# Two tiny weight reads ahead of ScalarE's table load, and the last two x tiles sent by ScalarE behind it

## The chip, the core and the metric

The kernel runs on one core of a Trainium2 chip. The metric is the device time of one execution in microseconds (us); lower is better. The engines are named as the profile names them: PE (TensorE, matrix products; PEld its weight loads), DVE (VectorE), ACT (ScalarE), POOL (GpSimd) and SP (SyncE, which here only issues transfers). ACT can issue transfers too, from a queue of its own (ACTq in the profile; SP's is SPq).

## The reference

One input x of 2048 tokens by 512 features goes through two branches, and a gate per token mixes them. Everything is bf16.

```python
x = A_x
g = sigmoid((x * gate_w).sum(-1, keepdims=True))
a = A_ref(x, wq, wk, wv, wo, beta)   # 32 heads of 16, 4 segments of 512 tokens:
                                     # softmax attention inside the segment, plus
                                     # a linear memory carried over the segments
b = B_ref(x, W_gate, W_up, W_down)   # relu(x @ W_gate) * (x @ W_up) @ W_down, F = 1792
return g * a + (1 - g) * b
```

What matters here is the very first step: q = x @ wq for the first 512 tokens, which needs x transposed (features on the partitions) and wq, both read from HBM.

## The kernel before

The program is recorded as a list of operations, each with the tiles it reads and writes. A scheduler class (`Sched`) places them one by one: the string `ORDER` holds one letter per operation, and each letter names a queue whose next operation is placed. From the tiles that an operation reads and writes, `add` derives what it must wait for, and `_waits` writes these waits into the engine's program, ahead of the instruction. Every engine runs its own program strictly in order, so an instruction that waits holds up all that stands behind it on that engine, transfers that it issues included. A transfer that writes a tile also waits for an earlier transfer into a tile of the same name (`need(t, False)` for each `t` in `r.dmaw`). Each transfer takes one of 16 semaphores (`s_dma0` to `s_dma15`), and the 17th use of one waits for the landing of the first.

The start of the program goes like this. The first 512 tokens of x are read as four tiles of 128 tokens (`load_x0(0)` to `load_x0(3)`, 128 KB each, into slots of the tile `hT`). PE turns each tile over in four 128x128 products with an identity (L449), and DVE and ACT copy the result from PSUM to `xT` (L454 and L456). Then PE computes q for the first segment in 32 matmuls of 256 columns (L552; the order of their pieces is set in `proj`): for each of the four 128-row pieces kt of wq, one matmul for each of four head groups. The 256 columns are either tokens 0 to 255 (x tiles 0 and 1) or 256 to 511 (x tiles 2 and 3). PE's order is: tiles 0 and 1 turned over; first token half with kt 0, then kt 1; tile 2 turned over; first half with kt 2; tile 3 turned over; first half with kt 3; then 16 matmuls for the second half. After that come k (L561), v (L559), the attention, and the feed-forward branch (L754).

SP reads x tiles 0 and 1, three pieces of wq, x tile 3, the fourth piece of wq, then wk, wv and the rest. ACT first loads its function table (a dummy `exp`, called "tab", which writes `rden` and so makes the table load happen early), and behind that it issues x tile 2: `load_x0(..., "act")` reads `rden`, so the transfer waits for "tab". Later ACT issues three tiny reads of 16 rows by 32 columns from the feed-forward weights into the tile `adT`, which is not used yet at that time; they are called `touch`. A queue of PE matmuls on constants (L441, L473) runs while the first tiles are on the way.

Of the kernel before, what the change touches and what calls it, by code (L numbers as in the profile page):

```python
# [21 lines left out]

LETTERS = "abcdefghijklmnopqrstuvwxyzABCDEFGHIJKLMNOPQRSTUVWXYZ0123456789"
ORDER = (
    "hafgbgbgfgbgfgbgfagbgfbhhhhgbhhhhijijhbttttbttttbhhhhijttttbhhhhijttttbttttcbtttbtDCttbttDbttbttbbtCbtbtFtbctIbItFbtbFJqbJtzJJtbEtxbtStGbvtGbzTvJtbMTq"
    "HtbJxvSbvSvbMvvcToqkvbLvoxtMTvbTvGTvlLvboqvoxvVMTvTvMTvTnlqVnvLoTvlxTMtWTtMmtTWtCTpqFvlSxtJtVJvTCvTtMyTVtTRqFvRtxvMTvJvpMvKTtSqzCvTTvMxTteMtrSeFTqATvx"
    "TvJetATttMeDTqJvxATtRvETvTvMyTqrAMTvxVQvAtrMUVUzATqUtAxTtpATtUtGTtHATqGvTxTvAtRtAvdHqMTtxTvATtTJttCTLqTvEKTtToxvdtvMTptCvTtSLqTErxSvAVtAtzTtTCvVTqATvM"
    "xtAdtRvEtLotdqAvpxCTtvTETvvTMKvTJqLvATxTvMvTdtMrzoqTpAvTxWvAvWMvtALTtAtHAqHvTAxTvosuPTMunTuPnpPqTuTxoXuTusuPuPTqPTOuTpJxuJTuuuXTquTxTsYuTPtPtPuTHXqTNu"
    "xYusvPuyPTuPTupTyRqXuuxSuTSvrNLTRqYuATxTJvATvvJvATvRLqvAxSuovMTvpTuMLvTqTArxuVQTvAUrUMTVBquATxuToutATpvTqSvxuATVtMTvUGvTOqVAvMTxvUAvYvJvMTKqTvoxvvMTpv"
    "TeMvTvTALvTeMqTvxTMvevBvMroeMTnqnvTxpATvvTAvovMTvATqLMvTxTvAvpMsvPtALtPTqADvTTxvPTtBtMrFTqTKJWvAxtWvAvtMvTDAtMTqTtAxtRtETvCtTtAvFtATLqTtBxtCTXttEtTsHu"  # L30
    "TPPTuPTqvXxJuJupvuMTquTxTsuTPuPtPtOTXqTGsxvPuPYPvuXyTMvTqTyRuuovxuTMpurRRqTAuxTtATuTJvtNKTuTGYTuATvouLqAprAxrQAUuUAUuBqtATxvUAtTouvHApqTAuxuuATTNuTvTB"
    "YvvMTLqTovxuMTvvuMnTqnpuToxJsuJPTuPvTPuTqTOvTvxYTMvpvMvvMTqvTxvMvsMvvTPqPTLvPTxvTvMvrMTqTAvTxvTAvMvvALTqAvxAvvMTTvMvTqTArTxMvBWAvWvTLAqTvxTAvAMTvvAvLq"
    "TAvTxMvTvTBvvMXTqvMTxTvXMTuuTquTxTuTuusvTPuPTMquxPuNXuuTqYrTxTTvAuAuTvTAuTLAqvAxuTAuuNTqYvTxTvMTvuMuTuTqrxvAuAvTuTAvTAvAqLuTxvuvNuYTuTvTMqTvMxvMvuuMTs"
    "qTPuPxTvPTuvXvMTvTvMTvTvLuqvxvMvvBvMTqvTAxuMvvNvLTvBYqrMTxTTvAvAvLTvTMvTvATLvAqAvxMvvAwMvTvBvMTwLTvTvvMvwLwrvAwAwwAwAvAwMwwAwwBwwwOwYOwwYwwwwwwOwwwYww"
    "wwwwwOwwwwwYNY"
)
BANKS = (
    "012312301230123023012302130231201320132013201301230210321032102310231023023020302013120312131213212301230213021301303120312031201201212012302301231231"
# [260 lines left out]
def build_kernel(nc, A_x, A_wq, A_wk, A_wv, A_wo, A_beta, W_g, W_u, W_d, gate_w, out):  # L299
    _, S, D = A_x.shape  # L300
    F = W_g.shape[1]
    assert D == 512 and S % 512 == 0 and F % 128 == 0
    NSEG, KT, NF, NT = S // 512, D // 128, F // 128, S // 128
    EPS, SCALE = 1e-6, 16 ** -0.5
    sc = Sched()
    T = {}
    with contextlib.ExitStack() as stack:
        for name, shape, dt in plan(S, D, F):
            T[name] = stack.enter_context(nc.sbuf_tensor(name, shape, dt))
        PL = stack.enter_context(nc.psum_tensor("psL", [128, 4, 512], F32))  # L310
        PA = stack.enter_context(nc.psum_tensor("psA", [128, 4, 512], F32))
        for st in sc.streams:
            sc.sem[st] = stack.enter_context(nc.semaphore(f"s_{st}"))
        program(sc, nc, T, PL, PA, A_x, A_wq, A_wk, A_wv, A_wo, A_beta, W_g, W_u, W_d, gate_w, out, NSEG, KT, NF, NT, EPS, SCALE)
        with nc.Block() as block:
            sc.emit(block)
    return sc


def program(sc, nc, T, PL, PA, A_x, A_wq, A_wk, A_wv, A_wo, A_beta, W_g, W_u, W_d, gate_w, out, NSEG, KT, NF, NT, EPS, SCALE):  # L320
    V = type("V", (), T)
# [16 lines left out]
    def act(fn, occ, **k):  # L338
        return op("act", fn, occ, **k)
# [15 lines left out]
    def load(eng, names, dst, src, nbytes, occ=460.0, reads=()):  # L355
        (lact if eng == "act" else lsp).append(dma(eng, lambda e, dst=dst, src=src: e.dma_start(dst, src), nbytes, occ=occ, reads=reads, writes=names, name="ld" + names[0]))  # L356
    x0 = A_x[0, 0:512, :].rearrange("(i p) d -> p i d", p=128)
    def touch(n, src):
        load("act", ["adT"], V.adT[0:16, 32 * n:32 * n + 32], src, 1024)
    def load_x0(i, eng="sp"):  # L360
        load(eng, [f"hT{i}"], V.hT[:, i, :], x0[:, i, :], 140000, reads=["rden"] if eng == "act" else [])

    def load_w(nm, w, src, kts):
        for kt in kts:
            load("sp", [f"{nm}{kt}"], w[:, kt, :], src[kt * 128:(kt + 1) * 128, :], 360000 if (nm, kt) == ("wk", 0) else 140000)
    load_x0(0)
    load_x0(1)
    load_w("wq", V.wq, A_wq, range(3))
    load_x0(3)
    load_w("wq", V.wq, A_wq, range(3, KT))  # L370
    lact.append(act(lambda e: e.activation(V.rden[:, 0:1], nc.const_aps.tensor(1.0, [128, 1], F32), ACT.Exp), 1500, writes=["rden"], name="tab"))
    load_x0(2, "act")
    sc.queue(0, lact)
    load_w("wk", V.wk, A_wk, range(KT))
    load_w("wv", V.wv, A_wv, range(KT))
# [529 lines left out]
```

## Time and profile before

| | |
|---|---|
| median of 3 runs | 264.53 us (264.4 to 264.64) |
| the profiled execution | 264.83 us |
| its span, from the first to the last instruction | 262.9 us |
| PE busy | 259.4 us, 99% of the span |
| DVE, ACT, POOL busy | 72%, 71%, 47% |
| HBM read and written | 9.87 MB and 2.11 MB |

All times inside the program count from the start of the span. A row of the timeline gives the start, the duration, the engine, the line of the kernel, the operation, its output and input tiles, and how many instructions were merged into the row; a bracket gives idle time ahead of it and what ended it. A row for a transfer's issue gives the time that the issuing queue was busy with it; when the data is there is told by the "us to landing" of the list of transfers, counted from the start of the issue.

### The profile page before, as it was taken

What the parts mean: (1) busy time and instruction counts of PE and PEld (TensorE: products, weight loads), DVE (VectorE), ACT (ScalarE), POOL (GpSimd) and SP (SyncE); (2) the same over time, 40 slices, a digit from 0 to 9 for tenths busy, and PEclk for the clock granted to TensorE, in tenths of its full rate; (3) what the DMA queues carried; (4) which work ended last, traced back from release to release, by engine and by line L of the source; (5) the groups of instructions that cost most, each with busy time, mean ns of one, the idle gap of its engine ahead of it and who ended that gap; (6) DMA issues with size and microseconds to landing.
All of it is one profiled execution on the core that took longest, in us unless ns stands there. A gap on an engine that the chain in (4) does not pass through costs nothing.

```text
span 262.9 us, 6637 instructions
## 1 busy us (share of the span) xinstructions
PE 259.4 (99%) x2761; PEld 115.5 (44%) x2761; DVE 189.3 (72%) x365; ACT 186.2 (71%) x163; POOL 122.7 (47%) x283
## 2 busy tenths in 40 slices
PE   8999999999999999999999999999999999999996
PEld 5543444434444444434444444444434444444444
DVE  4589878888894597888885898758973665577600
ACT  3598889888886877887876957777886755674021
POOL 3017645863655547845444456535654543343000
DMA  6979621533632311533212211010230000000011
GB/s 177 294 288 243 145 46 42 143 99 50 213 107 43 82 42 42 101 79 25 53 34 62 61 42 39 24 24 4 42 85 20 28 17 20 20 22 0 2 40 42
DMA packets 34685, 19.36 MB, mean 74 GB/s; under 512 B 24032, under 2 KB 34144, under 8 KB 34656
## 3 DMA queue, kind: packets, MB, share of 16 engines
q1 hardware_dynamic: 34416, 18.80, 28.6%
q8 instruction: 22, 0.36, 0.6%
q10 hardware_dynamic: 240, 0.13, 0.2%
q14 instruction: 7, 0.06, 0.1%
HBM read 9.87 MB, written 2.11 MB: 46 GB/s over the span
## 4 chain that ended last, share of the span: by engine, by line
PE 96%; DMA 1%; SPq 1%; issue 0%; DVE 0%
PE psA L754 39%; PE psA L793 19%; PE psA L561 9%; PE psL L662 9%; PE psA L694 7%; PE psA L786 5%; PE psA L559 5%; DMA wq<-in_A_wq_dram 1%; PE psA L624 1%; SPq L356 1%; PE psA L552 1%; PE psA L604 1%; DVE osb L802 0%
## 5 line engine op out<-in xcount | busy, mean ns | idle before, releaser
L671 POOL TENSOR_SCALAR_AFFINE_SELECT E<-E 64x256 bf16<-64x256 bf16 (+1 forms) x256 | 115.0, 459 | 115.4 <-ACT E L666 106.9
L666 ACT ACTIVATE E<-psL 128x2048 bf16<-128x2048 f32 x72 | 135.1, 1876 | 33.6 <-PE psL L662 33.2
L754 PE MATMUL psA<-xT,wu 128*128 128x512 bf16 x224 | 61.5, 380 | 0.0
L754 PE MATMUL psA<-xT,wg 128*128 128x512 bf16 x224 | 61.5, 380 | 0.0
L793 PE MATMUL psA<-wd,hT 128*128 128x512 bf16 (+2 forms) x238 | 58.8, 367 | 0.0
L765 DVE TENSOR_TENSOR hT<-psA,rl 128x512 bf16<-128x512 f32 x56 | 38.0, 682 | 15.1 <-PE psA L754 11.2
L793 PEld LDWEIGHTS psA<-wd,hT 128*128 128x128 bf16 x238 | 21.4, 98 | 24.3 <-issue 2.8
L754 PEld LDWEIGHTS psA<-xT,wu 128*128 128x128 bf16 x224 | 19.8, 98 | 25.2 <-issue 4.1
L754 PEld LDWEIGHTS psA<-xT,wg 128*128 128x128 bf16 x224 | 20.1, 98 | 24.4 <-issue 2.6
L704 DVE STREAM_TRANSPOSE Tn<-psA 128x512 f32<-128x512 f32 x32 | 21.4, 699 | 10.9 <-PE psA L694 10.6
L662 PE MATMUL psL<-qT,kp 32*128 32x192 bf16 (+7 forms) x512 | 28.7, 287 | 0.2 <-issue 0.2
L762 ACT ACTIVATE rl<-psA 128x512 bf16<-128x512 f32 x29 | 17.3, 596 | 15.0 <-PE psA L754 14.8
L763 DVE TENSOR_SCALAR rl<-psA 128x512 bf16<-128x512 f32 x27 | 18.5, 686 | 5.8 <-PE psA L754 5.6
L662 PEld LDWEIGHTS psL<-qT,kp 32*128 32x128 bf16 x512 | 8.3, 92 | 27.3 <-issue 9.7
L694 PE MATMUL psA<-E,vaug 64*17 64x128 bf16 (+7 forms) x512 | 18.7, 283 | 0.0
L694 PE MATMUL psA<-E,vsh 64*17 64x128 bf16 (+7 forms) x512 | 18.3, 283 | 0.0
L559 PE MATMUL psA<-wv,xT 128*128 128x512 bf16 x64 | 16.9, 379 | 0.0
L561 PE MATMUL psA<-xT,wk 128*128 128x512 bf16 x64 | 16.9, 379 | 0.0
L786 PE MATMUL psA<-wo,oT 128*128 128x512 bf16 (+2 forms) x68 | 16.5, 367 | 0.0
L803 ACT ACTIVATE osb<-psA,omg 128x512 bf16<-128x512 f32 (+1 forms) x8 | 5.4, 673 | 14.4 <-PE psA L786 13.1
L802 DVE TENSOR_SCALAR osb<-psA,omg 128x512 bf16<-128x512 f32 (+1 forms) x9 | 6.3, 702 | 12.5 <-PE psA L786 10.4
L694 PEld LDWEIGHTS psA<-E,vaug 64*17 64x17 bf16 x512 | 11.6, 86 | 7.6 <-issue 2.3
(73 smaller groups left out, 235.0 us busy)
## 6 DMA issues: line engine op xcount, KB each, us to landing
vsh<-vaug SPq DMA_DIRECT2D x8, 272.0 KB, 3.6
out_dram<-osb SPq DMA_DIRECT2D x15, 128.0 KB, 1.7
wg<-in_B_W_gate_dram SPq DMA_DIRECT2D x8, 224.0 KB, 5.4
wu<-in_B_W_up_dram SPq DMA_DIRECT2D x8, 224.0 KB, 5.9
osb<-in_A_x_dram SPq DMA_DIRECT2D x12, 128.0 KB, 2.2
wd<-in_B_W_down_dram SPq DMA_DIRECT2D x3, 512.0 KB, 4.5
wq<-in_A_wq_dram SPq DMA_DIRECT2D x4, 128.0 KB, 2.7
wk<-in_A_wk_dram SPq DMA_DIRECT2D x4, 128.0 KB, 3.5
```

Of the source, the lines that this page charges most:

```text
L559: ins = e.matmul(A(ep)[:, :], lhsT=V.xT[:, kt, tok + col * 128:tok + (col + 1) * 128], rhs=w[:, kt, :], start=(kt == 0), stop=(kt == KT - 1))
L561: ins = e.matmul(A(ep)[:, :], lhsT=w[:, kt, col * 128:(col + 1) * 128], rhs=V.xT[:, kt, tok:tok + 512], start=(kt == 0), stop=(kt == KT - 1))
L662: ins = q.matmul(PL[:, jj, o:o + 512 - 64 * c], lhsT=V.kp[r, kslot(s, G), c, :], rhs=V.qT[r, qslot(s, G), 64 * c:512], start=True, stop=Tr ...
L666: acts.append(act(lambda a: a.activation(V.E[:, e, :, :], PL[:, :, :], ACT.Exp, scale=SCALE), t_act(2048), reads=[f"bankL{b}" for b in ran ...
L671: pools.append(pool(lambda g, ap=ap, base=base: g.affine_select(out=ap, in_=ap, compare_op=ALU.is_ge, fill=0.0, base=base, pattern=[[0, 4] ...
L694: ins = q.matmul(A(eps[p])[32 * jj:32 * jj + 17, 64 * c:512], lhsT=v[:, 8 * G + 2 * jj + p, :], rhs=V.E[r, e, jj, o:o + 512 - 64 * c], sta ...
L704: ds.append(dve(lambda e, p=p, ep=eps[p]: e.transpose(V.Tn[:, p, :], A(ep)[:, :]), 706, writes=[f"Tn{p}"], name=f"tr{s}_{G}_{p}", ep=eps[p ...
L754: ins = e.matmul(A(ep)[:, :], lhsT=w[:, kt, f * 128:(f + 1) * 128], rhs=V.xT[:, kt, c * 512:(c + 1) * 512], start=(kt == 0), stop=(kt == K ...
L763: ("dve", lambda e, ep=eg, r=r: e.tensor_scalar(V.rl[:, r, :], A(ep)[:, :], 0.0, None, ALU.max), t_dve(512))],
L765: evs.append(dve(lambda e, ep=eu, r=r, hs=hs: e.tensor_tensor(V.hT[:, hs, :], A(ep)[:, :], V.rl[:, r, :], ALU.mult), t_dve(512), reads=[f" ...
L786: ins = e.matmul(A(ep)[:, 0:c1 - c0], lhsT=V.oT[:, o0 + G, i * 128:(i + 1) * 128], rhs=V.wo[:, G, c0:c1], start=st_ and G == 0, stop=sp_ a ...
L793: ins = e.matmul(A(ep)[:, 0:c1 - c0], lhsT=V.hT[:, slots[f], i * 128:(i + 1) * 128], rhs=V.wd[:, f, c0:c1], start=st_ and f == f0, stop=sp ...
```

## The change

The change writes the start of the loads in another order. ACT's queue gets two tiny reads, of 16 rows by 32 columns of wq and of wk, ahead of the table load. x tile 3 moves from SP to ACT, behind x tile 2. SP, without x tile 3, sends the four pieces of wq in a row. The table `ORDER` gets letters for the two added operations and the moved one.

```diff
-    "hafgbgbgfgbgfgbgfagbgfbhhhhgbhhhhijijhbttttbttttbhhhhijttttbhhhhijttttbttttcbtttbtDCttbttDbttbttbbtCbtbtFtbctIbItFbtbFJqbJtzJJtbEtxbtStGbvtGbzTvJtbMTq"
+    "haaafgbgbgfgbgfgbgfagbgfahhhhgbhhhhijijhbttttbttttbhhhhijttttbhhhhijttttbttttcbtttbtDCttbttDbttbttbbtCbtbtFtbctIbItFbtbFJqbJtzJJtbEtxbtStGbvtGbzTvJtbM"
...
     load_x0(0)
     load_x0(1)
-    load_w("wq", V.wq, A_wq, range(3))
-    load_x0(3)
-    load_w("wq", V.wq, A_wq, range(3, KT))
+    load_w("wq", V.wq, A_wq, range(KT))
+    touch(3, A_wq[0:16, 0:32])
+    touch(4, A_wk[0:16, 0:32])
     lact.append(act(lambda e: e.activation(V.rden[:, 0:1], nc.const_aps.tensor(1.0, [128, 1], F32), ACT.Exp), 1500, writes=["rden"], name="tab"))
     load_x0(2, "act")
+    load_x0(3, "act")
     sc.queue(0, lact)
```

One source line is added, so line numbers from 371 on grow by one in the kernel after.

ACT's program from its first instruction, before. `rden` is written by "tab", `hT` holds the x tiles, `adT` receives the tiny reads, and s_act, s_pe and s_dma are the semaphores of ACT, of PE and of transfers:

```order
L371 ACT_TABLE_LOAD
L371 ACTIVATE rden<-const-float32-1.0 128x1
L356 DMA hT<-in_A_x_dram 128x512 [waits s_act]
L456 ACTIVATE xT<-psL 128x256 [waits s_pe] x2
L456 ACTIVATE xT<-psL 128x2x128 [waits s_pe] x2
L356 DMA adT<-in_B_W_gate_dram 16x32
```

The same stretch of ACT's program after the change:

```order
L356 DMA adT<-in_A_wq_dram 16x32
L356 DMA adT<-in_A_wk_dram 16x32 [waits s_dma0]
L371 ACT_TABLE_LOAD
L371 ACTIVATE rden<-const-float32-1.0 128x1
L356 DMA hT<-in_A_x_dram 128x512 [waits s_act]
L356 DMA hT<-in_A_x_dram 128x512
L457 ACTIVATE xT<-psL 128x256 [waits s_pe] x2
L457 ACTIVATE xT<-psL 128x2x128 [waits s_pe] x2
L356 DMA adT<-in_B_W_gate_dram 16x32 [waits s_dma1]
```

Two tiny reads stand ahead of the table load, and the second waits on s_dma0, the semaphore of the first, since both write a tile of the name `adT`. Both x tiles that ACT sends, and its first copies of `xT`, stand behind that.

SP's program from its start, before:

```order
L356 DMA hT<-in_A_x_dram 128x512 x2
L356 DMA wq<-in_A_wq_dram 128x512 x3
L356 DMA hT<-in_A_x_dram 128x512
L356 DMA wq<-in_A_wq_dram 128x512
L356 DMA wk<-in_A_wk_dram 128x512 x4
L356 DMA wv<-in_A_wv_dram 128x512 x3
L356 DMA wv<-in_A_wv_dram 128x512 [waits s_dma0]
```

And after:

```order
L356 DMA hT<-in_A_x_dram 128x512 x2
L356 DMA wq<-in_A_wq_dram 128x512 x4
L356 DMA wk<-in_A_wk_dram 128x512 x4
L356 DMA wv<-in_A_wv_dram 128x512
L356 DMA wv<-in_A_wv_dram 128x512 [waits s_dma0]
L356 DMA wv<-in_A_wv_dram 128x512 [waits s_dma1]
L356 DMA wv<-in_A_wv_dram 128x512 [waits s_dma2]
```

The fourth piece of wq moves up by one place and x tile 3 is gone from SP. Since ACT's two tiny reads take two of the 16 semaphores, SP's waits for a semaphore's earlier use begin two transfers sooner. PE's order of instructions is the same in both kernels.

More of the change, by code (lines that the diff above doesn't have):

```diff
@@ L24 @@
 ORDER = (
-    "hafgbgbgfgbgfgbgfagbgfbhhhhgbhhhhijijhbttttbttttbhhhhijttttbhhhhijttttbttttcbtttbtDCttbttDbttbttbbtCbtbtFtbctIbItFbtbFJqbJtzJJtbEtxbtStGbvtGbzTvJtbMTq"
-    "HtbJxvSbvSvbMvvcToqkvbLvoxtMTvbTvGTvlLvboqvoxvVMTvTvMTvTnlqVnvLoTvlxTMtWTtMmtTWtCTpqFvlSxtJtVJvTCvTtMyTVtTRqFvRtxvMTvJvpMvKTtSqzCvTTvMxTteMtrSeFTqATvx"
-    "TvJetATttMeDTqJvxATtRvETvTvMyTqrAMTvxVQvAtrMUVUzATqUtAxTtpATtUtGTtHATqGvTxTvAtRtAvdHqMTtxTvATtTJttCTLqTvEKTtToxvdtvMTptCvTtSLqTErxSvAVtAtzTtTCvVTqATvM"
-    "xtAdtRvEtLotdqAvpxCTtvTETvvTMKvTJqLvATxTvMvTdtMrzoqTpAvTxWvAvWMvtALTtAtHAqHvTAxTvosuPTMunTuPnpPqTuTxoXuTusuPuPTqPTOuTpJxuJTuuuXTquTxTsYuTPtPtPuTHXqTNu"
@@ L29 @@
[L29 to L32, printed above, removed]
@@ L33 @@
-    "TAvTxMvTvTBvvMXTqvMTxTvXMTuuTquTxTuTuusvTPuPTMquxPuNXuuTqYrTxTTvAuAuTvTAuTLAqvAxuTAuuNTqYvTxTvMTvuMuTuTqrxvAuAvTuTAvTAvAqLuTxvuvNuYTuTvTMqTvMxvMvuuMTs"
-    "qTPuPxTvPTuvXvMTvTvMTvTvLuqvxvMvvBvMTqvTAxuMvvNvLTvBYqrMTxTTvAvAvLTvTMvTvATLvAqAvxMvvAwMvTvBvMTwLTvTvvMvwLwrvAwAwwAwAvAwMwwAwwBwwwOwYOwwYwwwwwwOwwwYww"
-    "wwwwwOwwwwwYNY"
+    "haaafgbgbgfgbgfgbgfagbgfahhhhgbhhhhijijhbttttbttttbhhhhijttttbhhhhijttttbttttcbtttbtDCttbttDbttbttbbtCbtbtFtbctIbItFbtbFJqbJtzJJtbEtxbtStGbvtGbzTvJtbM"
+    "TqHtbJxvSbvSvbMvvcToqkvbLvoxtMTvbTvGTvlLvboqvoxvVMTvTvMTvTnlqVnvLoTvlxTMtWTtMmtTWtCTpqFvlSxtJtVJvTCvTtMyTVtTRqFvRtxvMTvJvpMvKTtSqzCvTTvMxTteMtrSeFTqAT"
@@ new lines @@
+    "vxTvJetATttMeDTqJvxATtRvETvTvMyTqrAMTvxVQvAtrMUVUzATqUtAxTtpATtUtGTtHATqGvTxTvAtRtAvdHqMTtxTvATtTJttCTLqTvEKTtToxvdtvMTptCvTtSLqTErxSvAVtAtzTtTCvVTqAT"
+    "vMxtAdtRvEtLotdqAvpxCTtvTETvvTMKvTJqLvATxTvMvTdtMrzoqTpAvTxWvAvWMvtALTtAtHAqHvTAxTvosuPTMunTuPnpPqTuTxoXuTusuPuPTqPTOuTpJxuJTuuuXTquTxTsYuTPtPtPuTHXqT"
+    "NuxYusvPuyPTuPTupTyRqXuuxSuTSvrNLTRqYuATxTJvATvvJvATvRLqvAxSuovMTvpTuMLvTqTArxuVQTvAUrUMTVBquATxuToutATpvTqSvxuATVtMTvUGvTOqVAvMTxvUAvYvJvMTKqTvoxvvMT"
+    "pvTeMvTvTALvTeMqTvxTMvevBvMroeMTnqnvTxpATvvTAvovMTvATqLMvTxTvAvpMsvPtALtPTqADvTTxvPTtBtMrFTqTKJWvAxtWvAvtMvTDAtMTqTtAxtRtETvCtTtAvFtATLqTtBxtCTXttEtTs"
@@ new lines @@
+    "HuTPPTuPTqvXxJuJupvuMTquTxTsuTPuPtPtOTXqTGsxvPuPYPvuXyTMvTqTyRuuovxuTMpurRRqTAuxTtATuTJvtNKTuTGYTuATvouLqAprAxrQAUuUAUuBqtATxvUAtTouvHApqTAuxuuATTNuTv"
+    "TBYvvMTLqTovxuMTvvuMnTqnpuToxJsuJPTuPvTPuTqTOvTvxYTMvpvMvvMTqvTxvMvsMvvTPqPTLvPTxvTvMvrMTqTAvTxvTAvMvvALTqAvxAvvMTTvMvTqTArTxMvBWAvWvTLAqTvxTAvAMTvvAv"
+    "LqTAvTxMvTvTBvvMXTqvMTxTvXMTuuTquTxTuTuusvTPuPTMquxPuNXuuTqYrTxTTvAuAuTvTAuTLAqvAxuTAuuNTqYvTxTvMTvuMuTuTqrxvAuAvTuTAvTAvAqLuTxvuvNuYTuTvTMqTvMxvMvuuM"
+    "TsqTPuPxTvPTuvXvMTvTvMTvTvLuqvxvMvvBvMTqvTAxuMvvNvLTvBYqrMTxTTvAvAvLTvTMvTvATLvAqAvxMvvAwMvTvBvMTwLTvTvvMvwLwrvAwAwwAwAvAwMwwAwwBwwwOwYOwwYwwwwwwOwwwY"
@@ L36 @@
+    "wwwwwwwOwwwwwYNY"
 )
```

## The prediction

> **What bounds the kernel now.** I read the page first, then the chain that ended last, then the timeline of the first 14 us engine by engine, and last the landings of single transfers. The page says that the whole program is a string of PE work:
>
> ```profile
> span 262.9 us, 6637 instructions
> PE 259.4 (99%) x2761; PEld 115.5 (44%) x2761; DVE 189.3 (72%) x365; ACT 186.2 (71%) x163; POOL 122.7 (47%) x283
> ...
> PE 96%; DMA 1%; SPq 1%; issue 0%; DVE 0%
> ```
>
> Those are busy time by engine and, in the last line, the shares of the chain that ended last. PE is 96% of it, so whatever delays PE at the start delays the end by as much, and there are 262.9 - 259.4 = 3.5 us of PE idle in all to take back. The chain's first stretch (start, duration, what) and the waits of PE in the whole program (total, times, longest) tell where the little idle time lies:
>
> ```profile
> 3.62 3.52 DMA wq<-in_A_wq_dram
> 7.14 0.05 issue
> 7.19 2.36 PE psA L552 x20
> 9.54 3.02 PE psA L561 x14
> ...
> PE psA L552 <- DMA wq<-in_A_wq_dram: 0.2, 1, 0.2
> ```
>
> PE waits for one transfer in the whole program: the fourth piece of wq, 0.2 us. That is all that an earlier wq could win on PE. The timeline of PE:
>
> ```profile
> 0.84 2.29 PE L441 MATMUL psL<-const-bfloat16-1.0 128*128 128x512 bf16 x5 [0.84 <-PEq L890]
> 2.93 1.06 PE L449 MATMUL psL<-ident,hT 128*128 128x128 bf16 x8
> ...
> 4.21 1.88 PE L552 MATMUL psA<-xT,wq 128*128 128x256 bf16 x8
> 5.92 0.39 PE L449 MATMUL psL<-ident,hT 128*128 128x128 bf16 x4
> 6.15 0.60 PE L552 MATMUL psA<-xT,wq 128*128 128x256 bf16 x4
> 6.58 0.39 PE L449 MATMUL psL<-ident,hT 128*128 128x128 bf16 x4
> 7.19 2.36 PE L552 MATMUL psA<-xT,wq 128*128 128x256 bf16 x20 [0.22 <-DMA wq<-in_A_wq_dram]
> 9.38 3.19 PE L561 MATMUL psA<-xT,wk 128*128 128x512 bf16 x14
> ```
>
> The rows at 5.92 and 6.58 are x tiles 2 and 3 being turned over, and q is done when k starts at 9.38. The first eight q matmuls start one per (5.92 - 4.21) / 8 = 0.21 us, the last twenty one per (9.38 - 7.19) / 20 = 0.11 us: the same shape, at half the time. The issuing engines and the copies, from ACT's, DVE's and SP's timelines:
>
> ```profile
> 0.80 1.28 ACT L371 ACT_TABLE_LOAD   x1 [0.80 <-PEq L890]
> 2.10 0.20 ACT L371 ACTIVATE rden<-const-float32-1.0 128x1 f32<-128x1 f32 x1
> 2.33 0.38 ACTq L356 DMA_DIRECT2D hT<-in_A_x_dram  x1
> 3.81 0.66 ACT L456 ACTIVATE xT<-psL 128x256 bf16<-128x256 f32 x2 [1.52 <-PE psL L449]
> ...
> 7.01 0.33 ACTq L356 DMA_DIRECT2D adT<-in_B_W_gate_dram  x1
> ...
> 11.31 0.60 ACT L566 ACTIVATE kT<-psA 128x512 bf16<-128x512 f32 x1 [0.27 <-PE psA L561]
> ...
> 6.89 0.42 DVE L454 CAST xT<-psL 128x256 bf16<-128x256 f32 x1 [0.23 <-PE psL L449]
> ...
> 0.81 0.87 SPq L356 DMA_DIRECT2D hT<-in_A_x_dram  x2
> 1.73 1.37 SPq L356 DMA_DIRECT2D wq<-in_A_wq_dram  x3
> 3.14 0.43 SPq L356 DMA_DIRECT2D hT<-in_A_x_dram  x1
> 3.62 0.43 SPq L356 DMA_DIRECT2D wq<-in_A_wq_dram  x1
> ```
>
> The table load starts at once, x tile 2 leaves ACT at 2.33 and x tile 3 leaves SP at 3.14. How long such transfers take from issue to landing (last number of each row; from the lists of transfers issued around 1, 2.3 and 3.3 us, and of the whole program):
>
> ```profile
> hT<-in_A_x_dram SPq DMA_DIRECT2D x2, 128.0 KB, 2.0
> ...
> hT<-in_A_x_dram ACTq DMA_DIRECT2D x1, 128.0 KB, 2.8
> ...
> hT<-in_A_x_dram SPq DMA_DIRECT2D x1, 128.0 KB, 3.2
> ...
> gexpT<-gscr SPq DMA_DIRECT2D x16, 2.0 KB, 1.9
> ...
> out_dram<-osb SPq DMA_DIRECT2D x1, 32.0 KB, 1.5
> ...
> adT<-in_B_W_gate_dram ACTq DMA_DIRECT2D x1, 1.0 KB, 3.2
> adT<-in_B_W_up_dram ACTq DMA_DIRECT2D x1, 1.0 KB, 4.4
> ```
>
> They are in this order: x tiles 0 and 1, x tile 2, x tile 3, four small reads per segment, the smallest store, and two tiny reads of the kind that the change adds. A tiny read is no quick one: 3.2 and 4.4 us while much else is in flight, and nothing in the program lands in less than 1.5.
>
> **The change, part by part.** *The tiny read of wq* starts at 0.80, where the table load started. Its issue holds ACT's queue for 0.33 us, but what counts is its landing, because the tiny read of wk behind it waits for that, and ACT goes in order: table load, "tab", x tiles 2 and 3 and the copies of xT are queued behind this wait. No row shows a tiny read on idle transfer engines, so I bound it: from below by the store's 1.5 us, from above by the 3.2 of the tiny read of W_gate. The nearest rows are x tiles 0 and 1, issued in the same microsecond (2.0), and the small gexpT reads (1.9). I take 2.1, a little over both, since x tile 0 moves at the same moment: landed at 2.90.
>
> The Trainium skill, DMA: Bandwidth & Descriptors, section "Latency and other measured facts", puts the floor of a tiny transfer's HBM round trip at about 0.8 us, which with the rest as below would bring q's end to an estimated 9.5 us, no change at all. No row here comes near it.
>
> *The tiny read of wk* then takes 0.33 us of issue: 3.23. Nobody waits for its landing early.
>
> *Table load, "tab" and x tile 2* follow as before, 2.33 - 0.80 = 1.53 us from the start of the load to the issue of x tile 2: issue at 4.76 instead of 2.33, 2.43 later. *x tile 3* is issued after 0.38 us plus a gap of 0.05, at 5.19 instead of 3.14, 2.05 later. x tile 2 took 2.8 from ACT's queue and x tile 3 took 3.2 behind SP's; bounds for both 2.0 and 3.2. I take 2.8 and, for tile 3 behind tile 2 on one queue, 3.0: landed at 7.56 and 8.19.
>
> *ACT's first copies of xT* stand behind the issue of x tile 3 and start about 5.6 instead of 3.81. PE runs its first four q matmuls from 4.21 to about 5.1, waits some 0.9 us for the copy of kt 1, runs four more, and then waits for x tile 2 anyway, so this costs nothing on top, as long as the clock of PE doesn't mind (below).
>
> *PE from there.* x tile 2 at 7.6, plus what stands between the two tiles in PE's order, 6.58 - 5.92 = 0.66: x tile 3 is turned over from 8.26 (it landed at 8.19). From there the copies: DVE's ended at 6.89 + 0.42 = 7.31, 0.73 after PE began tile 3; the four kt 3 matmuls fit in that. Then 0.06 of handing over and 16 x 0.11 = 1.76: 2.55 in all. q is done at 8.26 + 2.55 = 10.81 instead of 9.38: 1.4 us later.
>
> *SP's four pieces of wq in a row*: the fourth is issued 0.48 earlier (3.14 instead of 3.62) and its queue holds one tile less. It costs nothing, and its gain, the 0.22 us wait on PE, is lost behind the later x tiles.
>
> *SP's waits on semaphores* now meet other transfers: the second and third piece of wv wait for the tiny reads, the fourth of W_gate for x tile 2, the second of W_up for x tile 3. Their issues on SP before:
>
> ```profile
> 5.99 1.86 SPq L356 DMA_DIRECT2D wv<-in_A_wv_dram  x4
> 7.89 1.86 SPq L356 DMA_DIRECT2D wg<-in_B_W_gate_dram  x4
> 9.80 1.86 SPq L356 DMA_DIRECT2D wu<-in_B_W_up_dram  x4
> ```
>
> At 0.47 us each, and 0.5 sooner without x tile 3, they are due at 6.0, 6.4, 8.8 and 9.8; what they wait for has landed at 2.9, at 5 to 6 (issued at 2.9), at 7.56 and at 8.19. Nothing, and PE reads wv from 13.27 on (row below) and the others later.
>
> *The later tiny reads on ACT.* The one of W_gate moves from 7.01 to about 8.6, and the one of W_up waits for its landing, ahead of ACT's second copy of kT. With 3.2 to 4.4 us it lands at 11.8 to 13.0; that copy, at 11.31 before, would be due at 12.7 with the shift. So 0 to 0.3 us on ACT. Its reader on PE is a v matmul four places into the row below, about 1 us after its start, 2.4 us after the copy ended at 11.91. It hides there; were that cover gone, the 0.3 would show.
>
> ```profile
> 13.27 1.89 PE L559 MATMUL psA<-wv,xT 128*128 128x512 bf16 x8
> ```
>
> The sum: +1.4 us for this chain, nothing to take it back later, since PE then works without waits for transfers. The profiled execution took 264.83, so it would take 266.2; it lies 0.3 over the median of the runs, 264.53, and the forecast goes with the median: 265.9. With the low bounds (1.5 and 2.0) x tile 2 would land at 6.16 and q end about 9.4, +0.0; with the 2.0 of x tile 0 for all three, +0.5. With the high ones (3.2 throughout) x tile 2 lands at 9.06 and q ends at 12.3, +2.9.
>
> **Rivals.** *PE stays at the slow pace.* Before, PE worked without a gap from 0.84 to about 5.8, and then the pace doubled, while the granted clock reads 1.00 all along (columns: stretch, sum, busy, count, clock, transfer share, GB/s):
>
> ```profile
> 0.84:5.80 4.96, 4.96 (x23) 1.00 0.72 197
> 5.80:9.50 3.70, 3.48 (x35) 1.00 0.87 264
> ```
>
> After the change there is a gap at 5.1, ahead of that point, and another until 7.6. If the doubling needs unbroken work, the eight turns (0.11 instead of 0.06) and 24 q matmuls (0.21 instead of 0.11) that remain could cost up to 8 x 0.05 + 24 x 0.10 = 2.8 us more; half of that, since the pace may rise on the way, gives +2.8 in all, 267.3. For it speaks the order of events, against it that PE still has most of the first 5 us busy. The Trainium skill, TensorE: Matmul & The Clock Gate, "What's actually happening", says that full clock follows about 3.4 us of sustained work, in a window that runs freely; an estimate by it is up to one more window at half pace, 1.7 us more. The 5 us before the doubling agree with such a window; what a broken one does no row shows.
>
> *The tiny read and the tiles land fast.* With 1.5 to 2.0 us for the tiny read and about 2.0 for the x tiles the result is +0.0 to +0.5, 264.5 to 265.0. For it speaks that two of the three transfers of the first two microseconds took 2.0; against it that ACT's own one took 2.8 and the tiny ones 3.2 or more.
>
> *It gains.* The tiny read wakes ACT's queue, or wq's memory, so that everything behind it comes quicker. To decide, x tile 2 would have to land by 5.9 and tile 3 by 6.5, when PE can take them; with the 2.0 of the fastest x tile this asks for the tiny read in 1.2 us. The gain is then capped at PE's wait of 0.22 us: 264.3, inside what can be told apart.
>
> **How the numbers follow.** A measurement of this kernel can tell about 0.2%, 0.53 us, from no change. The forecast chain, +0.9 to +2.2, has 0.62; the slow pace 0.16; fast landings 0.19, of which 0.15 stay within 0.53 and 0.04 are slower; a gain has 0.03, all of it over 0.2% only by something that the profile doesn't show. So slower 0.82, same 0.15, faster 0.03. The range goes from 264.9 (fast landings in part) to 267.4 (the high landings, or the slow pace at half its price).
>
> **What would show it.** In the profile after: a wait of about 2 us on ACT between its first two transfers; the table load at about 3.2 instead of 0.80; x tiles 2 and 3 issued at 4.8 and 5.2; PE idle before L450 on a transfer of x for about a microsecond and before L553 on ACT's copy; no PE wait for wq; k (L562) starting at 10.8 instead of 9.38, and from there the same spacing to the end. The prediction is wrong if the table load starts before 2.3, if x tiles land within 2.2 us of issue, or if the first q matmuls after the gap still take 0.21 us each.

## The result: 268.9 us, 1.6% slower

The changed kernel took 268.9 us (median of 4 runs, 268.73 to 269.23) against 264.51 (264.4 to 264.64): ratio 1.0163, 95% interval 1.015 to 1.0175. The direction was forecast, the size was not: 4.4 us instead of 1.4, and outside the range.

The page of the kernel after, its span, PE's line, the row of the granted TensorE clock in 40 slices (tenths, 9 is full; the page of before has no such row, since no change of the clock was recorded there) and the chain by engine:

```profile
span 267.5 us, 6605 instructions
PE 256.2 (96%) x2727; PEld 116.0 (43%) x2761; DVE 189.2 (71%) x365; ACT 186.3 (70%) x163; POOL 122.2 (46%) x283
...
PEclk9599999999999999999999999999999999999999
...
PE 93%; DMA 2%; issue 2%; ACT 1%; DVE 0%; ACTq 0%
```

PE's share of the chain falls from 96% to 93%, and in the second slice (6.7 to 13.4 us) PE's granted clock was about half. A reading of full clock is weaker evidence: it stands wherever no lower clock is recorded, and before the change PE's first matmuls ran at half the later pace with the clock read as 1.00. So I go by the pace of the rows below, and by the clock only where it reads 0.50. The chain's first 10 us, in order of time (start, duration, what):

```profile
0.81 1.92 DMA adT<-in_A_wq_dram
...
2.74 0.32 ACTq L356
...
3.10 1.28 ACT L371
...
4.39 0.21 ACT rden L371
...
4.62 4.24 DMA hT<-in_A_x_dram
...
8.91 0.61 PE psL L450 x4
9.52 0.85 PE psA L553 x4
```

This is the whole story of the change in one column: the tiny read of wq, the tiny read of wk that waited for it, the table load, the dummy exp, x tile 2, and only then PE. Before, the chain reached the last 20 q matmuls at 7.19. The two longest waits of PE in the whole program (total, times, longest):

```profile
PE psL L450 <- DMA hT<-in_A_x_dram: 2.4, 1, 2.4
PE psA L553 <- ACT xT L457: 1.0, 1, 1.0
```

PE's timeline, and then two of ACT's first rows and the landings of the two tiny reads and of x tile 2 and x tile 3 (last number):

```profile
4.35 0.60 PE L553 MATMUL psA<-xT,wq 128*128 128x256 bf16 x4 [0.21 <-DVE xT L455]
5.95 0.61 PE L553 MATMUL psA<-xT,wq 128*128 128x256 bf16 x4 [1.00 <-ACT xT L457]
8.91 0.61 PE L450 MATMUL psL<-ident,hT 128*128 128x128 bf16 x4 [2.35 <-DMA hT<-in_A_x_dram]
9.31 1.06 PE L553 MATMUL psA<-xT,wq 128*128 128x256 bf16 x4
10.17 0.63 PE L450 MATMUL psL<-ident,hT 128*128 128x128 bf16 x4
10.59 3.94 PE L553 MATMUL psA<-xT,wq 128*128 128x256 bf16 x20
...
17.48 0.40 PE L663 MATMUL psL<-qT,kp 32*128 32x512 bf16 x4
```

```profile
3.10 1.28 ACT L371 ACT_TABLE_LOAD   x1 [3.10 <-DMA adT<-in_A_wq_dram]
...
4.62 0.84 ACTq L356 DMA_DIRECT2D hT<-in_A_x_dram  x2
...
adT<-in_A_wq_dram ACTq DMA_DIRECT2D x1, 1.0 KB, 1.9
adT<-in_A_wk_dram ACTq DMA_DIRECT2D x1, 1.0 KB, 2.0
...
hT<-in_A_x_dram ACTq DMA_DIRECT2D x1, 128.0 KB, 4.2
...
hT<-in_A_x_dram ACTq DMA_DIRECT2D x1, 128.0 KB, 4.7
```

Look at the q matmuls: four at 4.35 in 0.60 us, four at 9.31 in 1.06 us, the same shape. The first group runs at the fast pace, so PE had already sped up, and it was slowed down again while it waited. The last row, the first attention scores (L662 before, L663 now), is my marker from here on, since a record or two of k's matmuls are missing in some traces: it started at 12.50 before and starts at 17.48, 5.0 us later. (The spans differ by 4.6; from the marker to the end the two traces differ by 0.4, which I don't explain: over all the kernels below that stretch lies between 250.0 and 250.6.)

### The profile page after: what moved, and what is told of

It is laid out like the page before. It is cut to its first block, busy times and chain, and to the rows that moved or that the text cites. A ratio compares the mean times of both kernels' runs of the same rounds, so it can differ in the third digit from the quotient of the medians.

```text
span 267.5 us, 6605 instructions
## 1 busy us (share of the span) xinstructions
PE 256.2 (96%) x2727; PEld 116.0 (43%) x2761; DVE 189.2 (71%) x365; ACT 186.3 (70%) x163; POOL 122.2 (46%) x283
## 4 chain that ended last, share of the span: by engine, by line
PE 93%; DMA 2%; issue 2%; ACT 1%; DVE 0%; ACTq 0%
PE psA L755 36%; PE psA L794 18%; PE psA L562 9%; PE psL L663 9%; PE psA L695 7%; PE psA L560 5%; PE psA L787 5%; PE psA L553 2%; DMA hT<-in_A_x_dram 2%; PE psA L625 1%; DMA adT<-in_A_wq_dram 1%; ACT E L667 1%; PE psA L605 1%; ACT L371 0%; PE psL L450 0%
## 5 line engine op out<-in xcount | busy, mean ns | idle before, releaser
L755 PE MATMUL psA<-xT,wu 128*128 128x512 bf16 x214 | 59.2, 380 | 1.6 <-issue 1.4
L755 PE MATMUL psA<-xT,wg 128*128 128x512 bf16 x213 | 59.0, 380 | 1.6 <-issue 1.4
L794 PE MATMUL psA<-wd,hT 128*128 128x512 bf16 (+2 forms) x232 | 57.6, 367 | 0.7 <-issue 0.6
L663 PE MATMUL psL<-qT,kp 32*128 32x192 bf16 (+7 forms) x512 | 28.6, 287 | 0.0
L663 PEld LDWEIGHTS psL<-qT,kp 32*128 32x128 bf16 x512 | 8.2, 92 | 27.0 <-issue 9.3
```

The costliest lines, as they stand in the source:

```text
L663: ins = q.matmul(PL[:, jj, o:o + 512 - 64 * c], lhsT=V.kp[r, kslot(s, G), c, :], rhs=V.qT[r, qslot(s, G), 64 * c:512], start=True, stop=Tr ...
L755: ins = e.matmul(A(ep)[:, :], lhsT=w[:, kt, f * 128:(f + 1) * 128], rhs=V.xT[:, kt, c * 512:(c + 1) * 512], start=(kt == 0), stop=(kt == K ...
L794: ins = e.matmul(A(ep)[:, 0:c1 - c0], lhsT=V.hT[:, slots[f], i * 128:(i + 1) * 128], rhs=V.wd[:, f, c0:c1], start=st_ and f == f0, stop=sp ...
```

## The experiments

The theories: (A) the wait of the second tiny read for the first holds up ACT's queue and is the root; (B) the two x tiles one behind the other on ACT; (C, G) the tiny reads by themselves cost, or help wq; (E, F) the x tiles landed late because they share the transfer engines with SP's stream, or because ACT's queue is slow; (D, H) PE's clock falls because PE is idle, and by what rule. The time of before beside the runs without the tiny reads, without the wait, with x tile 3 back on SP and with 24 filler matmuls is 264.62 us, beside the other four 264.59 us. Where operations are added, removed or moved to another engine, letters of `ORDER` change with them; these lines are not shown.

### Without the tiny reads

```diff
-    touch(3, A_wq[0:16, 0:32])
-    touch(4, A_wk[0:16, 0:32])
```

> The change without its two tiny reads; x tiles 2 and 3 still both on ACT, wq's four pieces still in a row. Theory A (the tiny read of wk waits for the landing of the tiny read of wq, and everything on ACT queues behind it): the table load starts at 0.8 again, x tile 2 is issued at 2.3 and x tile 3 at 2.75, both are there before PE asks for them at 5.9 and 6.6, time 264.2 to 264.8. Theory B (two x tiles one behind the other on ACT's queue land late beside SP's stream, 4 us or more as in the kernel after): x tile 2 lands at about 6.5 and x tile 3 at about 7.4, k starts 0.6 to 1.0 later than before, time 265.0 to 265.6.

Measured 264.55 us, ratio 1.0000 (0.9986 to 1.0015). ACT's row of the issue, the landing of x tile 2 and of x tile 3, and PE's last 20 q matmuls:

```profile
2.33 0.88 ACTq L356 DMA_DIRECT2D hT<-in_A_x_dram  x2
...
hT<-in_A_x_dram ACTq DMA_DIRECT2D x1, 128.0 KB, 2.8
...
hT<-in_A_x_dram ACTq DMA_DIRECT2D x1, 128.0 KB, 3.3
...
6.60 2.49 PE L551 MATMUL psA<-xT,wq 128*128 128x256 bf16 x20
```

Both tiles from ACT and four pieces of wq in a row cost nothing: theory B falls. They win nothing that the times show either, though in this trace PE no longer waits for wq.

### The tiny reads without the wait

```diff
-    touch(4, A_wk[0:16, 0:32])
+    load("act", ["oTt"], V.oTt[0:16, 0:32], A_wk[0:16, 0:32], 1024)
```

> The change whole, but the tiny read of wk goes into another tile that is unused then, so that it doesn't wait for the tiny read of wq. Theory A (the wait is the cost): the table load starts at about 1.6 (two issues of 0.4 and 0.33 ahead of it) instead of 3.1, x tile 2 is issued at about 3.1, time 264.5 to 265.8. Theory C (the tiny reads themselves, wherever they wait, are the cost, since they disturb ACT's queue): 267 or more.

Measured 264.86 us, ratio 1.0010 (0.9998 to 1.0023). ACT's rows:

```profile
0.81 0.41 ACTq L356 DMA_DIRECT2D adT<-in_A_wq_dram  x1
1.25 0.44 ACTq L356 DMA_DIRECT2D oTt<-in_A_wk_dram  x1
1.73 1.28 ACT L371 ACT_TABLE_LOAD   x1 [1.73 <-PEq L891]
...
3.25 0.84 ACTq L356 DMA_DIRECT2D hT<-in_A_x_dram  x2
```

One word in the source, the name of the tile that the second read writes, takes nearly the whole loss away. Theory A holds, and C falls: the table load starts 0.9 us late instead of 2.3, and that much PE's slow first matmuls still cover (in this trace their pace doubled only at about 6.5, when x tile 2 was there).

### One tiny read

```diff
-    touch(4, A_wk[0:16, 0:32])
```

> The change with the tiny read of wq alone ahead of the table load, none of wk, so nothing to wait for. Theory A: one issue of 0.42 delays the table load to 1.25, x tile 2 to 2.8, x tile 3 to 3.2; 264.3 to 264.9, no change. Theory G (the tiny read makes wq's pieces come sooner, and that helps): wq's pieces land in 2.1 to 2.8 instead of 2.7 to 3.2, and the time is 263.9 or less.

Measured 264.95 us, ratio 1.0013 (1.0004 to 1.0023): a loss of 0.1%, just over the expectation, and no gain. The pieces of wq landed in 2.4 to 3.8 us after their issue, no sooner than without tiny reads (2.7 to 3.2): theory G falls.

### The tiny reads behind the table load

```diff
-    touch(3, A_wq[0:16, 0:32])
-    touch(4, A_wk[0:16, 0:32])
     lact.append(act(...))          # "tab"
+    touch(3, A_wq[0:16, 0:32])
+    touch(4, A_wk[0:16, 0:32])
     load_x0(2, "act")
```

> The change whole, with the two tiny reads, wait included, behind the table load and the dummy exp instead of ahead of them. Theory A: ACT's queue issues the first tiny read at about 0.9 while the table loads, so the wait for its landing (1.9) runs beside the load, the second follows at 2.8, x tile 2 at 3.2 and x tile 3 at 3.65; they land at 6.1 to 6.9, close to the run without the wait: 264.5 to 265.5. If the queue can't issue beside the table load, the first tiny read goes at 2.1, x tile 2 at 4.7, and the time is 268 to 269 as in the change.

Measured 265.14 us, ratio 1.0031 (1.001 to 1.0053). ACT's table load and its first issues, and PE's wait:

```profile
0.81 1.28 ACT L369 ACT_TABLE_LOAD   x1 [0.81 <-PEq L891]
0.87 0.38 ACTq L356 DMA_DIRECT2D adT<-in_A_wq_dram  x1
...
2.87 0.32 ACTq L356 DMA_DIRECT2D adT<-in_A_wk_dram  x1
3.22 0.92 ACTq L356 DMA_DIRECT2D hT<-in_A_x_dram  x2
...
6.83 0.40 PE L450 MATMUL psL<-ident,hT 128*128 128x128 bf16 x4 [1.27 <-DMA hT<-in_A_x_dram]
```

The queue does issue beside the table load, so the wait costs 0.9 us of x tile 2's issue (3.22 instead of 2.33), as in the run without the wait. But here x tile 2 took 3.6 us to land instead of 2.9, PE's pace had doubled by 4.7, and PE stood for 1.3 us. That this costs more than the run without the wait is not shown, since the two intervals overlap. Nine of the ten executions lie between 264.8 and 265.64; one took 267.86, and it alone has a granted clock below 1.00 on average (0.994). The ratio of 1.0031 contains it, and by the medians the loss is 0.55 us. So the same kernel lost 2.7 us in one execution of ten, the one in which the clock fell.

### x tile 3 back on SP, the wait kept

```diff
-    load_w("wq", V.wq, A_wq, range(KT))
+    load_w("wq", V.wq, A_wq, range(3))
+    load_x0(3)
+    load_w("wq", V.wq, A_wq, range(3, KT))
...
-    load_x0(3, "act")
```

> Both tiny reads with their wait ahead of the table load, but x tile 3 is back on SP, where it was before. Theory A: x tile 2 is still issued at 4.6; alone on ACT's queue it lands in 2.8 to 3.4, at 7.4 to 8.0, q is done 3.2 later, k starts at 10.7 to 11.3 if PE's pace stays fast (time 265.8 to 266.5) and up to 2.2 later if it falls again (up to 268.7). Theory B (the move of x tile 3 is the cost): x tile 2 is no hindrance, 264.5 to 265.3.

Measured 267.61 us, ratio 1.0101 (1.0073 to 1.0129). x tile 2's issue and landing, and PE's wait:

```profile
4.70 0.36 ACTq L356 DMA_DIRECT2D hT<-in_A_x_dram  x1
...
hT<-in_A_x_dram ACTq DMA_DIRECT2D x1, 128.0 KB, 3.6
...
8.39 0.61 PE L451 MATMUL psL<-ident,hT 128*128 128x128 bf16 x4 [2.23 <-DMA hT<-in_A_x_dram]
```

About two thirds of the loss, 3.0 of 4.4 us, stays with x tile 3 where it was. The change loses some 1.4 us more. At the marker (15.92 here, 17.48 in the change) the two traces differ by 1.6: 0.5 from x tile 2, turned over at 8.39 instead of 8.91, and 1.0 from the last 20 q matmuls, 2.90 us instead of 3.94, since the clock was at half for 3.4 us here and for 6.8 there. That the second tile on ACT makes the first one land later is not shown: with the same two tiles on ACT, x tile 2 landed in 3.4 us in a run below.

### SP held back until x tile 3 is there

```diff
-  ... 360000 if (nm, kt) == ("wk", 0) else 140000)
+  ... 360000 if (nm, kt) == ("wk", 0) else 140000, reads=["hT3"] if (nm, kt) == ("wk", 0) else ())
```

> The change whole, but SP holds wk, and all behind it, until x tile 3 has landed, so that x tiles 2 and 3 don't share the transfer engines with SP's stream. Theory E (they landed in 4.2 and 4.7 us instead of 2.8 and 3.0 because they share the engines with wk and wv): issued at 4.6 to 4.7 they land in at most 3.0 and 3.3, PE turns tile 2 over at 7.5 to 7.8 instead of 8.9. The total is no better, since wk then comes after 11 us: 266.5 to 268.5. Rival F (ACT's queue is slow by itself at that time): 4 us or more again, 268.5 or more.

Measured 266.73 us, ratio 1.0080 (1.006 to 1.010). ACT's issue of x tiles 2 and 3, the landing, PE's rows around x tile 2 and up to k, and PE's busy time in a stretch (stretch, sum, busy, clock, share of the transfer engines, GB/s):

```profile
4.67 0.84 ACTq L356 DMA_DIRECT2D hT<-in_A_x_dram  x2
...
hT<-in_A_x_dram ACTq DMA_DIRECT2D x1, 128.0 KB, 2.1
...
6.00 1.03 PE L553 MATMUL psA<-xT,wq 128*128 128x256 bf16 x4 [0.59 <-ACT xT L457]
6.83 0.63 PE L450 MATMUL psL<-ident,hT 128*128 128x128 bf16 x4
...
8.53 3.02 PE L553 MATMUL psA<-xT,wq 128*128 128x256 bf16 x20
11.60 2.97 PE L562 MATMUL psA<-xT,wk 128*128 128x512 bf16 x13
...
3.00:6.40 3.40, 2.81 (x18) 1.00 0.72 203
```

The same transfer from the same queue at the same time lands in 2.1 us instead of 4.2 when SP's stream is out of the way. Theory E holds and F falls: in the change, x tile 2 was issued into the middle of wk, whose pieces had been issued from 3.6 on, with wv behind them. PE doesn't wait for wk, though it comes last: k starts at 11.60, right behind q. The marker is at 14.50, 3.0 us earlier than in the change; part of that is lost later, in a wait of 0.4 us for a transfer of x that stands behind the held stream on SP.

The rows show something else. The four q matmuls at 6.00 took 1.03 us, the slow pace, and PE kept it until about 9.9, with the clock read as 1.00 all the while. The pace had not doubled yet, while in the other nine traces it first doubled between 3.6 and 6.5. So a PE that waits can also get its fast pace late, and the granted clock doesn't show that. One of the four executions of the change (268.77 us) and one with x tile 3 back on SP (266.89 us) have a mean granted clock of 1.000 too; without a trace of them it stays open whether PE sped up late there.

### Filler on PE

```diff
+    def fill(m):                   # m matmuls of constants, 256 columns, into psL bank 0
+        ...
+    fill(4)                        # after the q matmuls of kt 0
+    fill(20)                       # after those of kt 1
```

> The change whole, with 4 and 20 matmuls of 256 columns on constants put on PE where it would wait (after the first four and after the second four q matmuls), into a PSUM bank that is free then; their result isn't used. Theory D (PE's clock falls because PE stands idle, and that costs 2.2 us of the 4.4): the granted clock stays 1.00, the 20 q matmuls after x tile 3 take 2.2 to 2.4 instead of 3.9 us, k starts at about 12.3 instead of 14.6, time 266.3 to 267.2. Rival: the clock falls all the same or the slow pace has another cause, 268.5 to 269.2.

Measured 267.40 us, ratio 1.0101 (1.0078 to 1.0124), a little above the expectation. PE's rows from x tile 2 on, with the marker:

```profile
8.97 0.40 PE L450 MATMUL psL<-ident,hT 128*128 128x128 bf16 x4
9.21 0.60 PE L562 MATMUL psA<-xT,wq 128*128 128x256 bf16 x4
9.70 0.40 PE L450 MATMUL psL<-ident,hT 128*128 128x128 bf16 x4
9.93 2.49 PE L562 MATMUL psA<-xT,wq 128*128 128x256 bf16 x20
...
15.38 0.39 PE L672 MATMUL psL<-qT,kp 32*128 32x512 bf16 x4
```

x tile 2 came at the same time as in the change (8.97 and 8.91), 24 matmuls of no use were added, and the marker stands at 15.38 instead of 17.48: 2.1 us earlier. By the ratios the gain is 1.0163 - 1.0101 = 0.6%, 1.6 us, the two being from different sets of runs. Theory D holds: four q matmuls take 0.60 us here and 1.06 in the change, and 1.6 to 2.1 us of the loss are PE's slow pace.

### Less filler

The same with `fill(14)` in place of `fill(20)`.

> As the run with filler matmuls on PE, but 14 instead of 20 in the long gap, so that PE is idle for about 0.9 us in a row ahead of x tile 2. Theory H (the clock follows PE's busy share over windows of 3.4 us; it fell after a window that was 57% busy and rose after one that was 80% busy): every window is over 70% busy, the clock stays at 1.00, k starts at about 12.3, 266.9 to 267.7. Rival (any gap of over half a microsecond makes it fall): granted clock 0.50 from 7 to 8 us on for at least 3.4 us, 268.2 or more.

Measured 266.64 us, ratio 1.0077 (1.0057 to 1.0097), below the expectation. PE kept the fast pace, but the test was not made as meant: x tile 2 landed in 3.4 us this time and was turned over at 8.16, and by the rows the filler ends at 8.21, so no gap of 0.9 us was left. The longest was 0.65 us, ahead of the second four q matmuls, and it did not drop the clock. What did is better read from the two runs in which it fell. The windows between its changes, the first of each run counted back from the fall, in the change and then in the run with x tile 3 back on SP (columns as before):

```profile
3.59:7.01 3.42, 1.76 (x14) 1.00 0.81 237
7.01:10.42 3.41, 1.51 (x11) 0.50 0.92 297
10.42:13.84 3.42, 3.42 (x20) 0.50 1.04 384
...
4.36:7.77 3.41, 1.30 (x9) 1.00 0.87 269
7.77:11.19 3.42, 2.80 (x18) 0.50 0.97 263
```

After 51% and 38% busy the clock fell, after 44% it stayed down, after 100% and 82% it rose. And it stayed down for 6.83 us in one and 3.42 in the other, two windows and one. That is not yet a rule by the busy share: in the run with SP held back PE was 83% busy from 3.00 to 6.40 (2.81 of 3.40 us), nearly a window if they are counted back from the doubling at 9.9, and the pace did not double behind it. Where the line runs stays open. The Trainium skill, TensorE: Matmul & The Clock Gate, "What's actually happening", gives a free-running window of 3413 ns and the half clock; these two traces agree with the length and with the half.

## Why the prediction was wrong

- *The tiny read's landing*: 2.1 us foretold, 1.92 measured. Right, and so was the choice of the row of x tile 0 (2.0) over the tiny reads of later on.
- *The wait and the queue behind it*: table load at 3.23 foretold and 3.10 found, x tile 2 issued at 4.76 and 4.62. Right; and by the run without the wait it is the root of nearly all of the 4.4 us.
- *ACT's first copies of xT*, "costs nothing on top, as long as the clock of PE doesn't mind": PE waited 1.00 us there, ahead of the wait for x tile 2, and the clock did mind: it fell after a window that held this wait and the start of the next.
- *The landing of x tiles 2 and 3*, 2.8 and 3.0 us: the first step that failed. It was mis-sized, and the high bound of 3.2 too. They took 4.2 and 4.7. I carried 2.8 over from a transfer issued at 2.33, when SP's stream was still short, to one issued in the middle of wk and wv. The rows of the same moment were there: SP's own pieces of wk and wv took 3.2 to 3.8 in the trace of before. Part of the miss can be chance: beside the same stream x tile 2 took 4.2 in two traces and 3.4 in a third. PE would have turned x tile 3 over at 8.26 by the sum; with the clock kept up by filler it was 9.70, 1.4 us later.
- *PE from there*, 2.55 us to the end of q: right with filler (9.70 to k's start at 12.26), wrong in the change, at half the clock. Its price, 2.1 us at the marker, lies under the rival's upper bound of 2.8. One of the signs of being wrong that I had named came true here: the first q matmuls after the gap still took 0.21 us each (0.85 for four in the chain).
- *The rivals*: the second step that failed. I priced the slow pace on top of the forecast wait at 267.3 and gave it 0.16, as one case among others. But with filler in place of the waits the slow pace is gone, so the waits are what makes PE slow: 1.0 and 2.4 us of them left two windows of 3.4 us 51% and 44% busy. The two should have been one case. The way was another, too: I had the doubling come late; in the trace of the change it came at 3.6, ahead of both waits, and the clock fell again at 7.0. The forecast 1.4, plus 1.4 of landing, plus 1.6 to 2.1 of clock is 4.4 to 4.9; measured are 4.4.
- *wq in a row, SP's waits, the later tiny reads*: no cost found. PE never waited for wq, and without the tiny reads the time is that of before.

## What to carry to other kernels

Before a transfer is put on a compute engine's queue, look at what it has to wait for there, write-after-write between two reads into one scratch tile included: the whole queue behind it pays the landing. A landing time belongs to the moment of issue, so take it from rows that are issued into the same stream, and leave room above it. And a stall early in a TensorE kernel is to be priced twice, as the time it lasts and as half a clock for the windows that follow, when it empties a good part of a 3.4 us window (here the clock fell after windows that were 51% and 38% busy).

## What the runs showed of the hardware

A transfer of 1 KB from HBM took as long as one of 128 KB issued at the same time (1.9 and 2.1 us). ACT's queue issued a transfer at 0.87 while the table load ran from 0.81 to 2.09. The same transfer, from the same queue at the same time, took 2.1 us with SP's stream held back and 3.4 to 4.2 beside it. PE, which started at 0.84 in every trace, first doubled its pace at 3.6 to 6.5 in nine traces, and at 9.9 in the one with a wait ahead of the doubling.
